# Weight loads in halves, two banks shared by two kinds of sums, and a new written order in a block of attention and spatial gating

## The chip, the cores and the metric

The kernel runs on one core of one Trainium2 chip. The metric is the device time of one execution in microseconds (us). A core has five engines with an instruction queue each: TensorE (PE in the profile; its weight loads are PEld), VectorE (DVE), ScalarE (ACT), GpSimd (POOL) and SyncE (SP), which here only issues DMAs. Engines run their queues in order and wait for each other by semaphores. TensorE writes its sums to eight banks of 128 x 512 float32, from which VectorE and ScalarE read.

## The reference

For 2048 rows of width 448, a vector c gives six modulation vectors; then an attention block and a gated mixer follow, each with a norm ahead and a residual behind:

```python
mod = (silu(c) @ w_mod)                     # sa, ca, ga, sb, cb, gb
h = layernorm(x) * (1 + ca) + sa
x = x + ga * attention(h)                   # 16 heads of 28, causal window of 256
h = layernorm(x) * (1 + cb) + sb
z = gelu(h @ w_in); z1 = z[:, :896]; z2 = layernorm(z[:, 896:])
g = w_sp @ z2 + b_sp[:, None]               # w_sp is 2048 x 2048: over the rows
x = x + gb * ((z1 * g) @ w_out)
```

All inputs and the output are bfloat16.

## The kernel before

The kernel first makes a list of operations in Python: each has a function that emits one or a few instructions (of TensorE, up to 64 matmuls), the operations that it depends on, and a claim on a buffer or a bank (`Hold`, with a `View` that lists the allowed choices). Nothing at run time chooses: a string, `PLAN`, holds one word for each operation, such as `p373.0`: the engine (p TensorE, a ScalarE, d VectorE, t GpSimd, s SP), the operation's number, and which choice each of its claims takes. `order()` reads the words from left to right, puts each operation at the end of its engine's queue, and adds a dependency on the previous holder of the claimed buffer. `count()` and `waits()` then make semaphore counts of it. So the order on each engine, the engine of an operation that could run on several, and the bank of each sum are all in that string, written once by a planner ahead of time. The numbers beside the operations (durations, priorities, `lat`) served that planner alone and do nothing when the kernel runs.

Rows are taken in 16 tiles of 128 (j, or t), and in four blocks of 512 (tb).

Front (to about 13 us): c goes through SiLU, the first modulation vectors are made, the first block of x is normed and transposed on TensorE. Small matmuls on constant data (L564) fill TensorE's waits there.

Attention. For each block, hT (transposed normed rows) comes from SP's transposing DMAs and gets its scale and shift (L731, on VectorE or GpSimd). TensorE makes Q (L762, L796), K (L820) and V (L840) into banks 6 and 7 (`bM`); they are copied out by ScalarE or VectorE (QT: L771 and L772, K: L832 and L833, V: L844 and L845). A copy of part of Q spread over zeros (QBD: L789 and L790, L814 and L815) lets one matmul serve eight heads for 64 queries. For each tile there are two halves of eight heads. Scores (L955) go to banks 0 to 3 together, and ScalarE takes their exponential (L911) into PW. Once a tile, two more matmuls make scores for eight heads (L966) in a bank of their own (`bC`, bank 5) with a short exponential (L911, 128 x 512). VectorE multiplies by the causal and window masks (L974) into PT. P.V (L1002) collects the 16 heads of a tile in one bank (`bO`, bank 4); the sums carry the softmax's denominator as a further column, so VectorE takes a reciprocal (L1016) and divides (L1018) into o_sb, which frees bank 4 for the next tile. SP transposes o_sb (`d_oT`), TensorE multiplies by w_o (L1028), VectorE adds the residual (L1032). Second norm: statistics (L628, L630, the power on GpSimd L632), the negated mean (L648), the norm (L643 or L650), a copy of its last columns (L655, L656), a transposition on SP (`d_hT`), and scale and shift for a block of four tiles (L1051 on ScalarE, L1053 on VectorE or GpSimd). w_o is scaled by ga (L600) ahead of L1028; L582 copies part of w_mod for L535.

Mixer, first half: z2 groups (L1122, GELU L1129 on ScalarE, statistics L628 and norm L1134 on VectorE), z1 groups (L1143, GELU L1151). They read w_in, which five DMAs load: three chunks of 128 rows (L432) and the last 64 rows twice (L434). Each pair of these groups needs pairs of banks (`bF`), freed by the GELUs.

Mixer, second half: w_sp @ z2 (L1168, 28 groups of 16 matmuls) with w_sp transposed by 32 DMAs from SP (`wspA` for the first half of the output rows, `wspB` for the second); VectorE adds the bias (L1172), GpSimd multiplies by z1 (L1175), TensorE multiplies by w_out (L1187), VectorE adds the residual (L1197), and SP or ScalarE stores. The first L1168 waits for all 16 z2 tiles and for wspA.

SP's queue holds loads, all transpositions and the stores in one order. An entry that waits for its source holds up those behind it.

The bank choices and the loads that the change touches:

```python
bO = View(banks, [(4,)])
bM = View(banks, [(6,), (7,)])
bC = View(banks, [(5,)])
bW = View(banks, [(0, 1, 2, 3)])
bF = View(banks, [(0, 1), (2, 3), (4, 5), (6, 7)])
```

Below stand the functions that the change touches, as a program prints them.

Of the kernel before, what the change touches and what calls it, by code (L numbers as in the profile page):

```python
# [12 lines left out]
d24 d22 p50.1 p59.3 p51.2 p58.0 p60.1 p62.0 a0 a3 a5 a7 a9 d23 d25 d26 d27 p40.1 p68.2 p74.3 p64.1 p52.0 p67.2  # L13
p53.3 p76.0 p49.3 p70.0 s1 s2 s4 d113 s6 s10 s8 a41 p45.0 p46 p47.1 p48 p73.2 p75.1 p63.2 t30 t31 t32 t35 t36
t33 d111 d114 t34 d112 t115 t37 a103 t29 t105 t38 d117.3 d116.2 p125.7 d86 d85 p128.0 p78.0 a129 a130 d106
d126 d127 d120 d121 d118 d119 a107 p83.1 p80.0 p81.1 p79.2 p77.0 p55.3 p72.2 p71.0 s12 d183 d181 p65.1 t104
p54.0 p149.1 p84.2 p140.5 p141 p150 a151 p82.1 p57.2 a142 t109 t110 t108 p137.7 p138 a139 p66.2 t122 d124.2
d123.0 p134.3 p131.6 p69.3 p56.0 p146.0 p147 p61.2 a132 d177 d184 d135 a136 s13 d243 d179 d178 d182 d180 t28
t185 t191 t187 t189 d245 d44 d241 d186.3 s11 p143.7 p370.0 a133 p164.1 p171.6 p172 d244 p165 d166 a148 p152.0
p144 d145 d173 d247 p153 d154 a371.0 p376.0 p155.1 p156 d157 a42 a377.4 p394.0 a395.1 a396 a170 t39 d380 d372  # L20
d246 d167 d374 p158.7 p159 a160 s15 p93.1 p94 d95 d248 d87 d88 d242 d397 p96.0 p97 d98 d378 s193 t188.1 s194
t190.2 s195 t192.0 s196 d197 d200 p401.0 a402.5 p174.1 p175 a176 p161.7 p162 p373.0 p89.0 p90 d91 d198 d92
a403 a43 p421.0 a422.6.0 t249 t253 d404 t251 t199 p375 p379 p381 d406 d382 d399 t252.2 d163 p217.0 p218 a219
a169 p210.1 p211 d212 p429.0 a430.0 p201.0 p202 a203 d168 p204.1 p205 a206 s14 d309 d383.2 p398.0 p400 p448.0
a449.2.1 s16 d426 s831 s258 t254.1 s259 d250.0 d255 d425 d432 d311 s384 s257 t256.3 s260 t100 t99 t261 t102
t262 t264 p226.0 p423.0 a424 p207.1 p227 p405 p208 d228 d305 p407 d408 d409.1 d306 s410 d101 d310 d431 a209
d215 d453 p456.0 p229.0 a457.1 d459 d214 d458 d452 p220.1 p221 p230 a231 p427.0 p428 s833 p475.0 p433 p434
d435 p223.0 p224 d225 d312 p450.0 a222 p232.1 d436.2 s437 d213 a476.3.2 d480 p483.0 d307 p233 d234 p235.0 p236
a451 a216 p477.0 p454.0 p455 a484.0 p501.0 d485 d486 d308 s21 s17 s834 p460 p461 d462 d479 d463.0 s464 a237
t263 p385.0 p386 d387 p411.1 p412 a478 p503.0 d413 t313 a502.6.0 p528.0 a504 d388 d505 d389 p481.0 p482 p487  # L30
p488 p271.0 p530.0 d489 d490.1 a529.2.1 d533 d506 d532 p272 a273 p509.0 a510.5 p268.1 p274.0 p275 d276 p269
d270 p507.0 p508 a531 p555.0 a556.3.2 p281.0 p265.1 p266 a267 d512 p282 p557.0 a558 a283 d511 p513 t317 t318.1
s323 t319 t320.2 s324 d314.0 s321 t315 t316.3 s322 t328 d279 d414 d560 p536.0 a537.1 p438.1 p439 d440 d280
p514 d515 d516.0 p287.0 p288 a289 p290.1 p291 a292 p563.0 a564.5 p238.0 p239 d278 p293.1 p534.0 p294 p535
p582.0 a240 p465.0 p466 d441 d442 d538 d415 d277 s20 s491 s830 s517 t390 d539 d391.2 t392 s393 a295 a583.4.0
# [215 lines left out]
def bass_adaLN_cond__sliding_block__mixer_gmlp__prompt_kernel(  # L251
# [14 lines left out]
    FH = 896  # L266
# [101 lines left out]
    sc = Sched()  # L368
    add = sc.add
    banks = Res(range(8), [])  # L370
    bO = View(banks, [(4,)])
    bM = View(banks, [(6,), (7,)])
    bA = View(banks, [(6,), (7,), (0,), (1,), (2,), (3,), (4,), (5,)])
    bL = View(banks, [(0,), (1,), (2,), (3,)])
# [325 lines left out]
    for tb in range(NB4):  # L700
# [33 lines left out]
        if tb == 0:  # L734
            for half in range(2):
                mine = {}
                for cp in range(2):
# [6 lines left out]
                    for k in range(2):  # L744
                        ch = cp + 2 * k
# [525 lines left out]
```

## Time and profile before

| | before |
|---|---|
| three timed runs | 276.37, 278.57, 280.68 us (median 278.57) |
| the profiled execution | 276.24 us |
| its span in the trace | 274.5 us |
| TensorE busy | 266.4 us (97%) |
| VectorE busy | 163.6 us (60%) |
| ScalarE busy | 121.5 us (44%) |
| GpSimd busy | 117.2 us (43%) |
| granted TensorE clock | 1.00 |

The span runs from the first instruction of the program to its last; the execution's own time has 1.7 us around it. Line numbers (L1002) are those of the kernel before, tensor names those of its program (ps: the banks). In a list of waits a row names who waited, for whom, how long in total, how often, and the longest. In the chain a row is a start, a duration and what ended last there. In a list of groups there stand line, engine, operation, output and inputs with shapes, the count, busy time in us, the mean of one in ns, and the idle time ahead. Matmuls overlap in TensorE's pipeline, so the mean of one is longer than its share of the busy time.

### The profile page before, as it was taken

The numbers are of one execution on the slowest core, as the hardware profiler recorded it, in microseconds if no ns is written. First come the engines' busy times: TensorE is split into PE (matmuls) and PEld (weight loads), VectorE is DVE, ScalarE is ACT, GpSimd is POOL, SyncE is SP. The second block draws the span as 40 slices with busy tenths as digits, with TensorE's granted clock in tenths as the row PEclk, the third lists the DMA queues.
The fourth block names the chain that finished last, engine by engine and source line by source line (L and its number), as shares of the span: only waits on it lengthen the run. The fifth ranks groups of instructions, "written<-read, shape, count | busy, mean of one in ns | idle before, by whom it ended". The sixth has DMA issues, their size and how long they took to land.

```text
span 274.5 us, 8392 instructions
## 1 busy us (share of the span) xinstructions
PE 266.4 (97%) x3741; PEld 154.1 (56%) x3751; DVE 163.6 (60%) x365; ACT 121.5 (44%) x142; POOL 117.2 (43%) x160
## 2 busy tenths in 40 slices
PE   7999998999999899999999999999999999999996
PEld 5877586678667676544544444444444444444453
DVE  3798999979899999949889301221212022153144
ACT  2599998899898789367766400000000000000000
POOL 7565467616483231488348003354453024062330
PEclk9999999999999999999999999999999999999999
DMA  7999844935431443659599996000000000001003
GB/s 216 320 222 168 109 102 116 106 94 115 114 61 43 127 61 69 175 109 155 96 173 201 191 192 112 0 0 0 2 0 0 0 2 0 33 17 52 17 33 117
DMA packets 67301, 25.54 MB, mean 93 GB/s; under 512 B 58497, under 2 KB 66178, under 8 KB 67266
## 3 DMA queue, kind: packets, MB, share of 16 engines
q1 hardware_dynamic: 66016, 24.02, 43.2%
q10 hardware_dynamic: 1250, 0.99, 1.3%
q8 instruction: 29, 0.48, 0.8%
q14 instruction: 6, 0.05, 0.1%
HBM read 9.01 MB, written 1.84 MB: 40 GB/s over the span
## 4 chain that ended last, share of the span: by engine, by line
PE 78%; DVE 12%; DMA 3%; ACT 2%; issue 2%; SPq 1%; DVEq 0%
PE ps L1168 35%; PE ps L1122 8%; PE ps L1143 8%; PE ps L1187 6%; PE ps L1002 5%; DVE PT L974 4%; PE ps L1028 4%; PE ps L820 3%; PE ps L955 3%; DMA x_sb<-in_A_x_dram 2%; PE ps L840 2%; PE ps L762 2%; DVE st_all L628 1%; DVE o_sb L1018 1%; DVE QBD L790 1%
## 5 line engine op out<-in xcount | busy, mean ns | idle before, releaser
L1175 POOL TENSOR_TENSOR z1T<-tmpg,z1T 128x512 bf16<-128x512 bf16 x28 | 32.0, 1152 | 77.7 <-DVE tmpg L1172 77.7
L1172 DVE TENSOR_TENSOR tmpg<-ps,bsp_bc 128x512 bf16<-128x512 f32 x28 | 19.0, 689 | 75.9 <-PE ps L1168 64.6
L911 ACT ACTIVATE PW<-ps 128x2048 bf16<-128x2048 f32 (+1 forms) x42 | 60.0, 1452 | 5.4 <-PE ps L955 3.7
L1168 PE MATMUL ps<-wspB,z 128*128 128x512 bf16 x219 | 49.7, 379 | 0.3
L1168 PE MATMUL ps<-wspA,z 128*128 128x512 bf16 x219 | 49.1, 379 | 0.4 <-issue 0.2
L632 POOL TENSOR_TENSOR rs_all<-mv_all,neghalf 128x1 f32<-128x1 f32 (+2 forms) x37 | 24.3, 676 | 33.1 <-DVE mv_all L630 33.1
L974 DVE TENSOR_TENSOR PT<-PW,mask 128x1024 bf16<-128x1024 bf16 x56 | 38.1, 704 | 0.2
L1168 PEld LDWEIGHTS ps<-wspA,z 128*128 128x128 bf16 x224 | 21.8, 98 | 26.6 <-issue 0.4
L1168 PEld LDWEIGHTS ps<-wspB,z 128*128 128x128 bf16 x224 | 21.9, 98 | 26.2
L1002 PE MATMUL ps<-Vaug,PT 128*128 128x32 bf16 x496 | 23.2, 177 | 1.4 <-DVE o_sb L1018 1.4
L1002 PEld LDWEIGHTS ps<-Vaug,PT 128*128 128x128 bf16 x496 | 21.3, 96 | 4.3 <-DVE o_sb L1018 2.4
L1122 PE MATMUL ps<-w_in,hT 64*128 64x448 bf16 x224 | 22.0, 349 | 0.0
L1187 PE MATMUL ps<-w_out_g,z1T 128*128 128x448 bf16 (+2 forms) x119 | 22.0, 342 | 0.0
L1143 PE MATMUL ps<-hT,w_in 64*128 64x512 bf16 x196 | 22.0, 376 | 0.0
L628 DVE BATCH_NORM_STATS2 st_all<-z 128x6 f32<-128x448 bf16 x32 | 18.4, 607 | 5.4 <-ACT z L1129 5.4
L628 DVE BATCH_NORM_STATS2 st_all<-x_sb 128x6 f32<-128x448 bf16 x32 | 19.4, 615 | 2.8 <-DMA x_sb<-in_A_x_dram 2.5
L1002 PE MATMUL ps<-Vaug,PW 128*128 128x32 bf16 x224 | 19.6, 176 | 0.0
L820 PE MATMUL ps<-hT,WQK 112*128 112x128 bf16 x256 | 17.4, 219 | 1.5 <-DVE KT L833 1.0
L1151 ACT ACTIVATE z1T<-ps 128x512 bf16<-128x512 f32 x28 | 14.6, 603 | 9.1 <-PE ps L1143 9.1
L1197 DVE TENSOR_TENSOR fin<-ps,x_sb 128x448 bf16<-128x448 f32 (+1 forms) x16 | 9.4, 611 | 14.7 <-PE ps L1187 11.4
L1002 PEld LDWEIGHTS ps<-Vaug,PW 128*128 128x128 bf16 x224 | 17.5, 96 | 1.1
L1129 ACT ACTIVATE z<-ps 128x896 bf16<-128x896 f32 x16 | 13.9, 913 | 7.9 <-PE ps L1122 5.4
(106 smaller groups left out, 351.8 us busy)
## 6 DMA issues: line engine op xcount, KB each, us to landing
wmodB<-in_w_mod_dram SPq DMA_DIRECT2D x1, 1568.0 KB, 14.7
out_dram<-fin SPq DMA_DIRECT2D x14, 112.0 KB, 1.7
x_sb<-in_A_x_dram SPq DMA_DIRECT2D x3, 448.0 KB, 7.5
w_in<-in_B_w_in_dram SPq DMA_DIRECT2D x3, 448.0 KB, 4.6
w_out_g<-in_B_w_out_dram SPq DMA_DIRECT2D x1, 784.0 KB, 5.0
bsp_bc<-in_B_b_sp_dram SPq DMA_DIRECT2D x1, 512.0 KB, 5.8
x_sb<-in_A_x_dram SPq DMA_DIRECT2D x2, 224.0 KB, 4.7
hT<-xn SPq DMA_TRANSPOSE x28, 3.0
```

Of the source, the lines that this page charges most:

```text
L628: st = [dve(0.62, lambda e, t=t, o=12 - 6 * (n - ci), s=s: e.bn_stats(st_all[:, slot, t, o:o + 6], s()), deps(t), prio) for ci, s in enume ...
L632: return pool(0.4 + 0.15 * len(tiles), lambda e: e.tensor_tensor(rs_all[:, slot, a:b], mv_all[:, slot, a:b, 1], neghalf[:, 0:b - a], ALU.pow),
L820: km = lambda g, kc, start, stop, h=h, t=t: lambda e: e.matmul(ps[:, h.slot[0], g * 128:(g + 1) * 128], lhsT=WQK[0:CP, kc, 16 + 4 * g:20 + ...
L911: ex = act(xdur, lambda e, out_ap=out_ap, in_ap=in_ap: e.activation(out_ap(), in_ap(), ACT.Exp, scale=SCALE), [s] + list(after), v - 8.0 + ...
L974: return lock_d(0.68, lambda e: e.tensor_tensor(cols(hp.slot[0] * 2048 + 1024 * k, [[256, 4], [128, 2], [1, 128]]), cols(at_w() + pad + at ...
L1002: fns.append(lambda e, hp=hp, hO=hO, hi=hi, bi=bi, kb=kb, hd=hd, nb=nb, a=at[hi][bi], p_of=p_of: e.matmul(ps[:, hO.slot[0], 32 * hd:32 * h ...
L1122: return lambda e, kc, p0, start, stop: e.matmul(ps[:, hs[t % 2].slot[hf], 0:D], lhsT=hT[p0:p0 + 64, kc, t * 128:(t + 1) * 128], rhs=w_in[ ...
L1143: return lambda e, kc, p0, start, stop: e.matmul(ps[:, hs[b // 2].slot[b % 2], :], lhsT=w_in[p0:p0 + 64, kc, ft * 128:(ft + 1) * 128], rhs ...
L1168: m = pe(16 * MMS, [lambda e, h=h, si=si, ft=ft, tb=tb: e.matmul(ps[:, h.slot[0], :], lhsT=z2[:, si, ft * 128:(ft + 1) * 128], rhs=(wspA i ...
L1172: a = dve(0.7, lambda e, h=h, ht=ht, tb=tb: e.tensor_tensor(tmpg[:, ht.slot[0], :], ps[:, h.slot[0], :], bsp_bc[:, tb * 512:(tb + 1) * 512 ...
L1175: u = pool(1.16, lambda e, ht=ht, ft=ft, tb=tb: e.tensor_tensor(z1T[tb][:, ft, :], tmpg[:, ht.slot[0], :], z1T[tb][:, ft, :], ALU.mult), [ ...
L1187: return [lambda e, ft=ft: e.matmul(ps[:, h.slot[0], 0:hi - lo], lhsT=z1T[t // 4][:, ft, (t % 4) * 128:(t % 4 + 1) * 128], rhs=w_out_g[:, ...
```

## The change

Three things are edited.

1. The three loads of 128 rows of w_in become six, each with half of the columns (0 to 895 and 896 to 1791). All readers still wait for all loads of w_in.
2. The sums of P.V (`bO`) and the scores for eight heads (`bC`) may each lie in bank 4 or 5, where before each had one bank.
3. `PLAN` is another string. The first 47 operations of TensorE, the first 13 of ScalarE, the first 18 of GpSimd and the first 11 of SP are the same, which is the front up to about 13 us. Behind it all five queues have another order, some operations another engine, and some claims another bank. From the first groups of L1168 on, TensorE and VectorE have the old order again.

The same operations are done with the same shapes, apart from the halved loads. Numbers of operations behind the loads go up by three, and line numbers behind the string by one.

By engine, the queues have these numbers of operations: TensorE 398 and 398, ScalarE 146 and 153, VectorE 365 and 376, GpSimd 156 and 138, SP 110 and 113.

```diff
 PLAN = """
-d24 d22 p50.1 p59.3 p51.2 p58.0 p60.1 p62.0 a0 a3 a5 a7 a9 d23 d25 d26 d27 p40.1 p68.2 p74.3 p64.1 p52.0 p67.2
...
+a0 t33 d27 s1 d30 d29 d28 d26 d25 p53.1 t34 p62.3 s2 t35 p54.2 t38 p61.0 s4 p63.1 p65.0 s6 a3 p43.1 a5 s10
...
 """
...
-    bO = View(banks, [(4,)])
+    bO = View(banks, [(4,), (5,)])
...
-    t_win_l = [load("d_win%d" % ch, "sp", 0.46, lambda e, ch=ch: e.dma_start(w_in[:, ch, :], B_w_in[ch * 128:(ch + 1) * 128, :]), (), -46.0 + 0.1 * ch)
-               for ch in range(3)]
+    t_win_l = [load("d_win%d%s" % (ch, "" if lo == 0 else "r"), "sp", 0.23, lambda e, ch=ch, lo=lo: e.dma_start(w_in[:, ch, lo:lo + FH], B_w_in[ch * 128:(ch + 1) * 128, lo:lo + FH]), (), -46.0 + 0.1 * ch)
+               for ch in range(3) for lo in (0, FH)]
...
-    bC = View(banks, [(5,)])
+    bC = View(banks, [(5,), (4,)])
```

123 lines of the change are left out of this document (62 added, 61 removed).

## The prediction

> **What bounds the kernel now.** I read the page first (busy time, chain by engine), then TensorE's waits, the chain in order of time, stretches, and groups of instructions by form. The page:
>
> ```profile
> span 274.5 us, 8392 instructions
> ...
> PE 266.4 (97%) x3741; PEld 154.1 (56%) x3751; DVE 163.6 (60%) x365; ACT 121.5 (44%) x142; POOL 117.2 (43%) x160
> ```
>
> TensorE is busy 97% of the span, and the diff takes none of its work away: both programs hand it the same matmuls. The time can fall only by what TensorE waits, and grows by every new wait. Its waits for other engines between 13 us, where the two programs' orders part, and 154 us, where the spatial product (L1168) starts:
>
> ```profile
> PE ps L1002 <- DVE o_sb L1018: 1.4, 2, 1.0
> PE ps L820 <- DVE KT L833: 1.0, 1, 1.0
> PE ps L925 <- ACT PT L911: 0.2, 1, 0.2
> ```
>
> Together 2.6 us, in four waits: that is what a better order behind the front can win, 0.9% of 276.24. Behind the first groups of L1168 the two programs have the same order on TensorE and VectorE, so the last 120 us only shift with the start of L1168. Where the waits sit, in the chain:
>
> ```profile
> 39.70 0.20 DVE PT L974
> 39.90 1.14 issue
> ...
> 42.49 1.07 PE ps L820 x16
> ...
> 90.77 0.46 PE ps L1002 x12
> ...
> 108.89 2.19 PE ps L1122 x22
> ...
> 144.80 9.06 PE ps L1143 x84
> ```
>
> Both long waits (ending at 42.49 and 90.77) stand behind VectorE. The 1.14 us of "issue" is a mask (L974) that took over a microsecond. From 90.77 us on TensorE is never released late. So two engines bound the middle together:
>
> ```profile
> 24.00:111.00 87.00, 84.52 (x2473) 61.44 (x2470) 82.92 (x176) 77.76 (x76) 43.05 (x53) 1.00 0.51 100
> 111.00:154.00 43.00, 42.87 (x432) 20.72 (x432) 34.78 (x91) 26.87 (x41) 25.83 (x46) 1.00 0.83 153
> ```
>
> After the length stand the busy times of PE, PEld, DVE, ACT, POOL, then the granted clock. In the attention (24 to 111 us) TensorE is busy 84.5 of 87 us, VectorE 82.9, ScalarE 77.8; in the mixer's first half VectorE has 8 us of air and ScalarE 16. The clock is 1.00 and stays out of the sum.
>
> **The change part by part.** The order view gives VectorE 11 more instructions, ScalarE 7 more, GpSimd 18 fewer. Means of the groups concerned:
>
> ```profile
> L974 DVE TENSOR_TENSOR PT<-PW,mask 128x1024 bf16<-128x1024 bf16 x56 | 38.1, 704 | 0.2
> ...
> L628 DVE BATCH_NORM_STATS2 st_all<-x_sb 128x6 f32<-128x448 bf16 x26 | 15.9, 616 | 0.2
> ...
> L790 DVE COPY QBD<-qT 32x512 bf16<-32x512 bf16 x11 | 4.0, 364 | 1.5 <-ACT qT L771 1.3
> ...
> L845 DVE CAST Vaug<-ps 128x448 bf16<-128x448 f32 x6 | 3.7, 613 | 0.1
> ...
> L772 DVE CAST qT<-ps 128x512 bf16<-128x512 f32 x4 | 2.7, 685 | 0.6 <-PE ps L762 0.6
> L1053 DVE TENSOR_SCALAR hT<-hT,modT 128x512 bf16<-128x512 bf16 x4 | 2.1, 513 | 0.0
> L833 DVE CAST KT<-ps 128x512 bf16<-128x512 f32 x3 | 2.0, 658 | 0.0
> L731 DVE TENSOR_SCALAR hT<-hT,modT 112x512 bf16<-112x512 bf16 x4 | 1.5, 399 | 0.0
> L650 DVE TENSOR_SCALAR xn<-x_sb,rs_all,nm_all 128x448 bf16<-128x448 bf16 x4 | 1.5, 374 | 0.5 <-DMA hT<-xn 0.5
> ...
> L655 DVE COPY xn<-xn 128x64 bf16<-128x64 bf16 x3 | 1.3, 443 | 0.0
> L648 DVE TENSOR_SCALAR nm_all<-mv_all,rs_all 128x1 f32<-128x1 f32 x6 | 1.2, 203 | 0.5 <-POOL rs_all L632 0.5
> ...
> L600 DVE TENSOR_TENSOR wo_g<-wo_g,gg_sb 112x448 bf16<-112x448 bf16 x1 | 0.6, 580 | 0.0
> L582 DVE COPY wmodE<-wmodB 112x512 bf16<-112x512 bf16 x2 | 0.4, 256 | 0.0
> ...
> L815 DVE COPY QBD<-qT 32x256 bf16<-32x256 bf16 x2 | 0.4, 194 | 0.0
> ```
>
> VectorE takes over from GpSimd two of L731 (0.80 us), one of L1053 (0.51), one of L600 (0.58), two of L648 (0.41), three of L650 (1.12) and four of L655 (1.77), and from ScalarE two of L815 (0.39), one of L833 (0.66) and one of L845 (0.61). It gives two of L582 (0.51) to GpSimd, two of L772 (1.37) and two of L790 (0.73) to ScalarE. Sum: 6.85 - 2.61 = +4.2 us, all ahead of L1168. How much of it lies ahead of a given instruction follows from the order view, each instruction at its group's mean:
>
> (1) The K eviction (L833) that TensorE waits for until 42.49 us; it frees one of the two banks that K has, and the next L820 needs it. Newly ahead of it on VectorE are one L628, three L648 net, one L600, two L815, two L650, one L833 and one L790, 4.0 us; no longer ahead are two L582, one L772 and one mask, 1.9 us; a pair of smaller ones cancels. So VectorE comes 2.0 us later by this count, while TensorE's matmuls ahead of that L820 are the same. Bounds for the wait: 3.0 us (1.0 now and all that is added) and 0 (if the slow mask's 1.14 us and as much again come back). I take 2.0, nearer the counted end: +1.0 us.
>
> (2) The second bank. Tile 10's sums of P.V lie in bank 4 in both programs; tile 11's go to bank 5 in the changed one, so its first L1002 no longer waits for the division (L1018) of tile 10. That takes off the wait of 1.0 us that ends at 90.77. The smaller one of its kind, 0.4 us, lies between tiles 0 and 1, which alternate now as well. Late next are the masks of tile 11, which stand beside that division in VectorE's queue; VectorE has 0.5 us more ahead of it than before. Bounds -1.4 and 0; I take -1.0. Seven of 16 tiles change bank; the others wait as now. In return the eight-head scores (L966) share a bank with sums:
>
> ```profile
> L911 ACT ACTIVATE PW<-ps 128x512 bf16<-128x512 f32 x14 | 8.4, 599 | 0.8 <-PE ps L966 0.8
> ```
>
> Their exponential keeps the bank for 0.6 us, so a P.V group right behind it would wait up to that, and none where other matmuls stand between, as the order has it: 0.
>
> (3) GpSimd's relief. Masks stretch where GpSimd works beside them; over all 56:
>
> ```profile
> L974 DVE TENSOR_TENSOR PT<-PW,mask x56: 616/682/1414, 31.1 to 110.3; 128x1024 bf16<-128x1024 bf16 x56
> ```
> ```profile
> L650 POOL TENSOR_SCALAR xn<-x_sb,rs_all,nm_all 128x448 bf16<-128x448 bf16 x17 | 14.6, 858 | 4.8 <-DVE nm_all L648 4.3
> L1053 POOL TENSOR_SCALAR hT<-hT,modT 128x512 bf16<-128x512 bf16 x11 | 8.8, 809 | 11.2 <-DMA hT<-xn 11.2
> L731 POOL TENSOR_SCALAR hT<-hT,modT 112x512 bf16<-112x512 bf16 x8 | 8.7, 1098 | 10.4 <-DMA hT<-xn 10.4
> ```
>
> Mean 704 against least 616 ns is 4.9 us of stretch. Up to 111 us GpSimd loses three L731 (3.3 us), three L650 (2.6) and small ones, some 8 of its 43 us: a fifth, so about 1.0 us of stretch comes back. Bounds 0 and 4.9; I take 1.0, half of it reaching TensorE: -0.5 us. The two L582, new on GpSimd, cost there between 0.26 us each (their VectorE row) and 0.70 (times 1098/399, L731's ratio); their reader (L535) ends no TensorE wait above. [...]
>
> (4) The end of the attention. Ahead of the last mask VectorE has 1.7 us more, less the 1.0 of (3). ScalarE has 0.7 us more ahead of the last long exponential; the last short one now stands behind it. TensorE's order puts mixer groups (L1122) between the last P.V groups as cover. Bounds 0 and +1.7; I take +0.5.
>
> (5) The mixer's first half. Six of the L1053 kind (scale and shift of the second norm) go to ScalarE.
>
> ```profile
> L1051 ACT ACTIVATE hT<-hT,modT 128x512 bf16<-128x512 bf16 x1 | 0.8, 814 | 0.0
> ```
> ```profile
> DVE st_all L628 <- ACT z L1129: 5.4, 6, 3.0
> ```
> ```profile
> 149.04 4.25 DVE L1134 TENSOR_SCALAR z<-z,mv_all,rs_all 128x896 bf16<-128x896 bf16 x10
> ```
>
> That is 4.9 us more on ScalarE, which has 16 us of air, but they queue between the GELUs that free TensorE's banks: a wait of up to 0.81 us each time, 4.9 in all, none if the spare banks hold. VectorE has 4.2 - 1.7 = 2.5 us more to do between the last mask and the last L1134, against 5.4 us in which it now waits for GELUs. Its last L1134 ends at 153.29, only 0.6 us before TensorE's L1143 does (153.86), and L1168 needs all of them. Bounds 0 and 2.5 - 0.6 = +1.9 from VectorE; I take +0.7 for both engines.
>
> (6) The w_in loads.
>
> ```profile
> w_in<-in_B_w_in_dram SPq DMA_DIRECT2D x3, 448.0 KB, 4.6
> ```
> ```profile
> w_in<-in_B_w_in_dram SPq DMA_DIRECT2D x2, 224.0 KB, 3.9
> ```
>
> Six of 224 KB for three of 448 KB: six landings of 3.9 us for three of 4.6, and three more issues on SP. The last half stands next to tile 10's o_sb transposition, which follows a division at about 91 us; the first reader of w_in is L1122 at 108.89. Cover 13 us or more, cost 0; without the cover 3 x (7.8 - 4.6) = 9.6 us at most. Transpositions behind a load wait less, but none of them ends a TensorE wait above. [...]
>
> Sum: +1.0 - 1.0 - 0.5 + 0.5 + 0.7 = +0.7 us. The profiled execution took 276.24 us (span 274.5 and 1.7 around it), so 276.9. It stands 2.3 us below the median of the three timed runs (276.37 to 280.68), and runs of the changed kernel will spread alike; halfway to the median gives 276.9 + 1.2 = 278.1 us.
>
> **The rivals.** (a) The waits go: VectorE gets its stretch back ahead of the K eviction, and the second bank takes its 1.4. Then -1.6 (a K wait of 1.0 left) to -2.6: 273.6 to 274.6 against 276.24. [...] Against it: VectorE's queue is longer at every point that I counted, by 0.5 to 4.2 us.
>
> (b) The other side: the handover to L1168 decides. VectorE's new queue puts work on landed transpositions (L650, L655, L1053) among the statistics; if one waits, all behind it waits. It costs time once VectorE is late by more than the 0.6 us above, and 2% (5.6 us) once by 6.2, that is if it keeps its 5.4 us of waits, does the 2.5 of new work and loses another 2 to 3 on landings: 282 and over. Against it: the waits of now fall on GELUs whose TensorE order is nearly the same, and the new work can fill them.
>
> (c) SP's queue.
>
> ```profile
> 135.09 7.31 SPq L465 DMA_TRANSPOSE wspA<-in_B_w_sp_dram  x5
> ...
> 143.78 1.29 SPq L465 DMA_TRANSPOSE wspA<-in_B_w_sp_dram  x1
> ```
> ```profile
> wspA<-in_B_w_sp_dram SPq DMA_TRANSPOSE x16, 4.3
> ```
>
> Between the last hT transposition and the end of wspA stand seven issues now, nine in the changed order. At up to 1.46 us each (7.31/5) the last is issued at 143.8 + 2.9 = 146.7 and lands at 151, 3 us before L1168. If the last norm is 5 us late, L1168 is 2 us late: 279.
>
> (d) The change does nothing: the waits only move: 276.2, within the forecast's range.
>
> **How the numbers follow.** Forecast (-1.0 to +2.5 around 276.9, (d) included) 0.63; (a) 0.22; (b) 0.10; (c) 0.05. Faster or slower by 2% of 278.57 is 5.6 us, about what a measurement of this kernel can tell from no change. (a) gets there only with every run at the low edge: faster 0.03. (b), and a third of (c) with runs at the high edge: slower 0.12. Within: 0.85. The range goes from (a)'s 274.6 for a run at the low edge to the forecast's +2.5 on the median, 281.1, and 0.7 for (c): 281.8.
>
> **What would show it.** In TensorE's waits: the one for L1018 near 91 us gone, the one for L833 near 42 us there and about 2 us long. VectorE's busy time up by some 3 us with the masks' mean below 704 ns; GpSimd's down by over 10. L1168 starting 0.7 us later, within -1 and +2.5. Wrong if TensorE waits for w_in, if L1168 starts past 158, or if TensorE waits over 2 us for ScalarE's share of L1053.

## The result, and the profile after

The changed kernel is slower by half a per cent: median 278.94 us over 20 runs (276.16 to 281.95) against 276.89 over 20 runs of the kernel before (275.87 to 280.68); ratio 1.0051, 95% interval 1.0026 to 1.0076, that is +1.4 us (0.7 to 2.1). The ratio leaves out the slow executions (over 1.5% above the fastest of their program: three of these 20, two of before's), so it is not that of the two medians. By the bound of 2% that is no change. The profiled execution took 280.08 us, 3.84 more than the one of before; as worked out below, 2.4 of these belong to that execution and not to the change.

Lines of the changed kernel are one higher than before (L1018 is L1019). Its page, TensorE's waits from 13 to 158 us, the masks, and the first weights of the spatial product with their first and last start:

```profile
span 278.4 us, 8397 instructions
...
PE 269.7 (97%) x3741; PEld 156.7 (56%) x3751; DVE 164.3 (59%) x376; ACT 127.4 (46%) x149; POOL 106.2 (38%) x142
```
```profile
PE ps L1123 <- ACT z L1130: 0.9, 1, 0.9
PE ps L1003 <- DVE o_sb L1019: 0.5, 1, 0.5
PE ps L821 <- DVE KT L834: 0.5, 1, 0.5
PE ps L841 <- DVE x_sb L1033: 0.4, 1, 0.4
PE ps L1003 <- issue: 0.3, 1, 0.3
PE ps L821 <- DVE Vaug L846: 0.2, 1, 0.2
PE ps L1169 <- issue: 0.2, 1, 0.2
PE ps L956 <- ACT PW L912: 0.2, 1, 0.2
```
```profile
L975 DVE TENSOR_TENSOR PT<-PW,mask 128x1024 bf16<-128x1024 bf16 x56 | 37.3, 688 | 0.5 <-ACT PW L912 0.4
```
```profile
L1169 PEld LDWEIGHTS ps<-wspA,z x224: 96/98/99, 157.7 to 226.3; 128*128 128x128 bf16 x112
```
```profile
L1168 PEld LDWEIGHTS ps<-wspA,z x224: 95/98/98, 153.8 to 222.4; 128*128 128x128 bf16 x112
```

The wait of 1.0 us near 91 us is gone, the K wait has halved to 0.5 instead of doubling, and a wait of 0.9 us in the mixer (L1123) is new. GpSimd is down by 11.0 us and ScalarE up by 5.9, but VectorE only by 0.7. The last two rows (after, before) show L1169 starting 3.9 us later. The waits have grown only from 2.6 to 3.0 us (without the row of L1169, which the kernel before has as well), so the list of waits does not tell where 3.9 us went.

What tells it is how late TensorE is. For each group of matmuls I take its start in the trace and subtract the work of all groups ahead of it, each matmul at the spacing that it has when nothing holds it (216 ns for L1168, 95 ns for L1122, 25 ns for L1002, and so on). What is left is TensorE's lateness, and only its rise between two places counts. Places are given in us of TensorE's work; its clock time is 4 to 10 us later. The profiled executions, first those with the order of before in the attention (e8, e10 and e12 are told in the text):

```
                       late  rise from .. to (us of TensorE's work)
                       at 6   6-36 36-37.5 37.5-84 84-92 92-110 110-132.5 132.5-133.5 133.5-260
before                 4.55   0.36   1.10  -1.07   0.94  -0.13    0.22     0.02       0.27
e11 before again       4.21   0.36   0.03   0.63   0.94  -0.12    0.21     0.03       0.27
e1 halves              5.34   0.52   1.26  -1.09   0.94  -0.12    0.21     0.03       0.27
e2 both banks          4.29   0.40   0.11   0.23   0.83  -0.12    0.21     0.03       0.27
e9 banks, K ahead      6.04   0.36   1.13  -0.41   0.75  -0.12    0.21     0.03       0.27
e4 new mixer           4.17   0.35   0.11   0.74   0.93   0.12    0.21     0.03       1.11
after                  6.96   0.66   0.67  -0.71   0.05   0.87    0.22     1.12       0.28
e5 after again         5.24   0.40   0.47  -0.49   0.02   1.17    0.22     1.26       0.28
e7 pair turned back    7.59   0.71   0.64  -0.73   0.15   1.34    0.22     1.43       0.29
e3 new attention       4.78   1.57   0.95  -0.02   0.03   1.45    0.22     0.03       0.26
e6 mixer mended        4.23   0.96   0.86  -0.73   0.02   1.12    0.22     0.03       0.26
e13 VectorE relieved   5.43   0.43   0.44  -0.66  -0.01   1.14    0.22     0.03       0.26
e14 ScalarE relieved   4.40   1.09   0.68  -0.73  -0.02   1.20    0.21     0.03       0.27
```

The front up to 6 us of work is the same in both programs but for VectorE's order, and there the two profiled executions differ by 2.4 us. TensorE waits 1.1 us for w_mod in after and 0.6 in before, where the last of its four loads lands at 7.8 and at 6.8 us. And its matmuls on constant data (L564 of before) start 213 ns apart until 4.6 us in both, but from 7.7 us on 109 ns in before and still 213 until 12.0 us in after; why is not shown, the granted clock is 1.00 in both. Behind the front the new order wins 0.9 us at 84-92 (the second bank), loses 1.0 to 1.6 at 92-110 (end of the attention) and 1.1 to 1.4 at 133 (last tiles of the mixer). For the two profiled executions: 2.41 in the front, 0.30 at 6-36, -0.07 at 36-84, -0.89, +1.00 and +1.10 make 3.85 of the 3.84 us.

Two sums of columns matter for what follows. Over 6-84 the new order's seven executions rise by 0.9 in the mean and the old order's six by 0.85, so up to there the orders are even. Over 84-110 the new order rises by 0.92 (after) to 1.49 and the old by 0.63 to 1.05: most of what the second bank wins at 84-92 is given back by the end of the attention. The clear loss of the change is the one at 133.

### The profile page after: what moved, and what is told of

It reads as the page before. It is cut to its first block, busy times and chain, and to the rows that moved or that the text cites. A ratio compares the mean times of both kernels' runs of the same rounds, so it can differ in the third digit from the quotient of the medians.

```text
span 278.4 us, 8397 instructions
## 1 busy us (share of the span) xinstructions
PE 269.7 (97%) x3741; PEld 156.7 (56%) x3751; DVE 164.3 (59%) x376; ACT 127.4 (46%) x149; POOL 106.2 (38%) x142
## 4 chain that ended last, share of the span: by engine, by line
PE 78%; DVE 13%; DMA 4%; ACT 3%; issue 1%; SPq 0%
PE ps L1169 35%; PE ps L1188 8%; PE ps L1144 6%; PE ps L1123 6%; PE ps L1003 5%; PE ps L956 4%; PE ps L1029 4%; PE ps L821 3%; PE ps L763 3%; DVE PT L975 3%; DVE st_all L629 2%; DMA wmodA<-in_w_mod_dram 2%; DMA hT<-xn 2%; PE ps L841 2%; ACT PW L912 1%; PE ps L565 1%
## 5 line engine op out<-in xcount | busy, mean ns | idle before, releaser
L1169 PE MATMUL ps<-wspB,z 128*128 128x512 bf16 x219 | 49.7, 379 | 0.3
L1169 PE MATMUL ps<-wspA,z 128*128 128x512 bf16 x219 | 49.1, 379 | 0.4 <-issue 0.2
L633 POOL TENSOR_TENSOR rs_all<-mv_all,neghalf 128x1 f32<-128x1 f32 (+2 forms) x37 | 25.8, 710 | 49.7 <-DVE mv_all L631 47.2
L975 DVE TENSOR_TENSOR PT<-PW,mask 128x1024 bf16<-128x1024 bf16 x56 | 37.3, 688 | 0.5 <-ACT PW L912 0.4
L1169 PEld LDWEIGHTS ps<-wspA,z 128*128 128x128 bf16 x224 | 21.8, 98 | 26.6 <-issue 0.4
L1169 PEld LDWEIGHTS ps<-wspB,z 128*128 128x128 bf16 x224 | 21.9, 98 | 26.2
L1003 PEld LDWEIGHTS ps<-Vaug,PT 128*128 128x128 bf16 x496 | 22.9, 96 | 5.3 <-issue 1.1
L1003 PE MATMUL ps<-Vaug,PT 128*128 128x32 bf16 x496 | 25.2, 177 | 0.5 <-DVE o_sb L1019 0.5
L1123 PE MATMUL ps<-w_in,hT 64*128 64x448 bf16 x224 | 22.5, 349 | 0.9 <-ACT z L1130 0.9
L1003 PE MATMUL ps<-Vaug,PW 128*128 128x32 bf16 x224 | 20.6, 176 | 0.3 <-issue 0.3
L1003 PEld LDWEIGHTS ps<-Vaug,PW 128*128 128x128 bf16 x224 | 17.8, 96 | 1.9
L821 PE MATMUL ps<-hT,WQK 112*128 112x128 bf16 x256 | 18.1, 219 | 0.7 <-DVE KT L834 0.5
L956 PEld LDWEIGHTS ps<-qT,KT 32*128 32x128 bf16 (+1 forms) x1344 | 13.4, 90 | 7.1 <-ACT PW L912 4.2
```

The costliest lines, as they stand in the source:

```text
L633: return pool(0.4 + 0.15 * len(tiles), lambda e: e.tensor_tensor(rs_all[:, slot, a:b], mv_all[:, slot, a:b, 1], neghalf[:, 0:b - a], ALU.pow),
L821: km = lambda g, kc, start, stop, h=h, t=t: lambda e: e.matmul(ps[:, h.slot[0], g * 128:(g + 1) * 128], lhsT=WQK[0:CP, kc, 16 + 4 * g:20 + ...
L956: fm.append(lambda e, hm=hm, qi=qi, key=key, kn=kn, lo=lo, hi=hi, col=col, p0=p0, t=t, j=j: e.matmul(ps[p0:p0 + kn, hm.slot[t], col:col + ...
L975: return lock_d(0.68, lambda e: e.tensor_tensor(cols(hp.slot[0] * 2048 + 1024 * k, [[256, 4], [128, 2], [1, 128]]), cols(at_w() + pad + at ...
L1003: fns.append(lambda e, hp=hp, hO=hO, hi=hi, bi=bi, kb=kb, hd=hd, nb=nb, a=at[hi][bi], p_of=p_of: e.matmul(ps[:, hO.slot[0], 32 * hd:32 * h ...
L1123: return lambda e, kc, p0, start, stop: e.matmul(ps[:, hs[t % 2].slot[hf], 0:D], lhsT=hT[p0:p0 + 64, kc, t * 128:(t + 1) * 128], rhs=w_in[ ...
```

## The experiments

Theories ahead of the first four: a Queue theory (the new order queues work behind VectorE and ScalarE), a Load theory (halved loads hold up SP), a Front theory (the new program's first loads land later). Ahead of the later ones the Queue theory is called order theory, and the landing theory says that late landings of one execution made the loss. In most experiments the written string is two lines shorter than in the changed kernel, so the attention's waits there read L1001, L819, L954 for L1003, L821, L956. Cuts of `PLAN` leave out words in between and, in places, the choice behind the point. In expectations L657, L1046 and L1055 are the pieces that the trace of the changed kernel has as L656, L1045 and L1054.

**e1: halves alone.** The changed program with one bank each and the `PLAN` of before, in which each of the three loads stands twice:

```diff
-s17 s834 ... s18 p594 ... s19 p641.0
+s17 s18 s837 ... s19 s20 p597 ... s21 s22 p644.0
```

> The order of before with the six half loads, each second half issued right behind its first. Queue theory (the +1.4 us of the changed kernel comes from waits behind VectorE and ScalarE at the end of the attention and from the last transposition of the mixer): 0 us against before, within 0.5, since no TensorE wait ends with a load. Load theory (three more loads hold up the transpositions behind them on SP's queue): +0.7 to +1.5 us. Front theory (the new program's first loads land later): 0 us.

Measured: 277.23 us, ratio 1.0002 (0.9967 to 1.0036). TensorE never waits for w_in and the table's rises are those of before. The loads cost nothing behind their cover.

**e2: the second bank alone.** `PLAN` of before, with the new choices of bank.

```diff
-    bO = View(banks, [(4,)])
+    bO = View(banks, [(4,), (5,)])
...
-    bC = View(banks, [(5,)])
+    bC = View(banks, [(5,), (4,)])
```

> The order of before, whole loads, with the bank 4 or 5 that the changed kernel gives each sum of P.V and each eight-head score. Queue theory: the TensorE wait of 1.0 us for the division (L1018) at 90.8 us goes and the small one near 31 us too; -1.0 us (between -1.4 and -0.6). Its rival, that the masks of tile 11 are late next: 0 us, with a wait of TensorE for L974 at the same place. Front theory says nothing against either.

Measured: 276.96 us, ratio 0.9996 (0.9962 to 1.0030). TensorE's waits between 84 and 95 us:

```profile
PE ps L954 <- DVE KT L832: 1.0, 1, 1.0
PE ps L1001 <- DVE o_sb L1017: 0.4, 1, 0.4
```

The wait for the division is gone, and a score (L955 of before) waits 1.0 us for a K eviction that VectorE ends at 91.91 us. The rise at 84-92 is 0.83 against 0.94: the bank alone moves the wait to the next piece in the same queue.

**e3 and e4: half of the new order each.** e3 has the new words to the end of the attention (746 of 1178), then all that is left in the order of before; e4 the reverse, with the last 426 words as in the changed kernel. Both have the halves and both banks. At e3's seam:

```diff
 s761 p778.1 s372
-p855.0 d783 a775 d737 t812 p779 p856.1
+a775 p779 t812 p855.0 p856.1 p857 d737
```

> The changed kernel up to its first mixer group (L1123 of the changed program) and the order of before for every operation left. Queue theory: the loss of 1.1 us in the mixer goes, the bank's gain (-1.1) and the loss at the end of the attention (+1.2) stay: +0.3 us against before (0 to +0.8). Front theory: as much as the changed kernel, +1.4 us, or more, as the new front is in it, and TensorE's second modulation matmuls start about 1 us later than in before.

> The order of before up to its first mixer group, then the changed order for every operation left, six half loads. Queue theory: the loss in the mixer alone, +0.9 us (+0.5 to +1.3), with a TensorE wait ahead of the mixer group of tiles 12 to 15 behind the transposition of tile 15. Front theory: 0 us or less, since the front is the one of before.

Measured: e3 277.78 us, ratio 1.0007 (0.9978 to 1.0036); e4 277.97 us, ratio 1.0012 (0.9971 to 1.0053). Neither interval excludes zero or half of the loss, but the traces part the places: e3 has the gain at 84-92 and the loss at 92-110, e4 neither. e4 lacks the loss at 133 in its profiled execution and has another one later, the bias. Waits of e4's VectorE and TensorE, 150 to 200 us:

```profile
DVE tmpg L1171 <- DMA bsp_bc<-in_B_b_sp_dram: 12.6, 1, 12.6
```
```profile
PE ps L1167 <- DVE tmpg L1171: 0.7, 1, 0.7
```

In the new order of SP the bias load stands behind seven more transposing loads of w_sp than before (28 instead of 21). VectorE waits 12.6 us for it, and TensorE waits 0.7 us for VectorE to empty a bank. In the changed kernel itself VectorE waits 11.0 us for the bias, but L1169 starts later there and TensorE does not wait.

**e5, e6, e7, e8: the new program again, and three ways to mend it.** e5 is the changed kernel. e6 makes two moves: on GpSimd the scaling of w_out goes behind the last tile's statistics, and on SP the bias load goes ahead of 16 transposing loads of w_sp:

```diff
-p1007.0 t802 t917 s798 d947 ... s850 s822 s842
+p1007.0 t917 t802 s798 s822 d947 ... s850 s842
```

e7 turns one pair of the attention's last scores and exponentials back:

```diff
-p780 ... p774 ... a781 ... a775
+p774 p780 ... a775 a781
```

e8 has the new words up to the long score of tile 13 (668 words) and then the order of before:

```diff
 a721 d578 d728
-p745.0 d529 d723 p656 p705 p369.1
+t807 d808 t529 s530 t809 s503 s681
```

> The changed kernel itself, once more, as the measure for the three others of this group and as a test of what of its loss belongs to the order and what to one execution. Order theory (the new order queues work behind VectorE and ScalarE): the profile has the same losses at the same places, TensorE 0.8 to 1.5 us later between 92 and 111 us by waits for exponentials, and L1123 waiting about 0.9 us near 143 us for L1055 behind the last transposition; median 1.0 to 1.8 us above the kernel before. Landing theory (the loss of the profiled execution was late landings, w_mod's at 7.9 us and the last hT transposition's 4.1 us): both absent in another execution, the span within 1 us of before's 274.5, median within 0.7 us of before.

> The changed kernel with two moves: the scaling of w_out (L1046) that ran on GpSimd beside the last tile's copy L657 on VectorE (1.04 beside 1.01 us) stands behind that tile's statistics, and the load of the bias goes to SP right behind the last hT transposition (it landed at 167.9 us). Order theory: L657 of tile 15 takes 0.2 to 0.4 us, the transposition starts 0.6 to 0.8 us earlier, the wait near 143 us falls from 0.9 to 0.1 or 0.3, no wait for the bias can occur; TensorE 0.7 to 1.1 us less late at 150 us than the changed kernel, median 0.7 to 1.1 us below it. Landing theory: L657 is shorter, but the wait near 143 us comes or goes with the landing (2.4 or 4.1 us) of the last transposition; median within 0.4 us of the changed kernel's.

> The changed kernel with one pair turned back to the order of before at the end of the attention: the short score of the second last tile and its short exponential (0.59 us) ahead of the long score and the long exponential (1.88 us) of the last tile. Order theory, in the form that this pair makes the loss: the rise of TensorE's lateness between 92 and 111 us falls from 0.9 to 0.4 or less, median 0.4 to 0.8 us below the changed kernel. In the form that the whole sequence from tile 13 on has too little between a score and the next: the rise stays at 0.8 to 1.2, median within 0.3 us. Landing theory: no difference outside the interval.

> The new program up to the long score of tile 13 (near 98 us), then everything that is left in the order of before; both banks, loads in halves. Order theory: it keeps the gain at tile 10 (no rise of TensorE's lateness at 86 us, -1.0) and has none of the two later losses (the rise between 92 and 111 us 0.3 or less, none near 143 us): 0.7 to 1.2 us less late at 150 us than the kernel before if the front is equal, median 0.3 to 1.0 us below before. Landing theory: equal to before within 0.4 us. Third possibility, that the early part of the new order loses as well (rises by 63 us of work, 0.4 to 0.8 in the run with the new attention): equal to before or up to 0.8 us above it.

Measured: e5 278.90 us, ratio 1.0058 (1.0026 to 1.0089); e6 277.61 us, 1.0025 (0.9986 to 1.0064); e7 278.99 us, 1.0084 (1.0050 to 1.0119); e8 280.20 us, 1.0081 (1.0039 to 1.0122).

e5 settles what belongs to the order: both late losses come back (1.17 and 1.26), the lateness of the front does not (5.24). The loss at 133 in e5, from the timelines of VectorE, GpSimd, SP and TensorE; a row is start, duration, engine, and in brackets the idle time before it:

```profile
134.49 1.01 DVE L656 COPY xn<-xn 128x64 bf16<-128x64 bf16 x1 [1.25 <-POOL xn L651]
```
```profile
134.42 1.04 POOL L1045 TENSOR_TENSOR w_out_g<-w_out_g,gg_sb 128x448 bf16<-128x448 bf16 x1
...
139.89 1.65 POOL L1054 TENSOR_SCALAR hT<-hT,modT 128x512 bf16<-128x512 bf16 x2 [3.92 <-DMA hT<-xn]
```
```profile
135.53 1.21 SPq L466 DMA_TRANSPOSE hT<-xn  x1
```
```profile
141.64 3.20 PE L1123 MATMUL ps<-w_in,hT 64*128 64x448 bf16 x32 [1.07 <-POOL hT L1054]
```

The last tile's norm ends in a copy of 64 columns on VectorE. GpSimd has just begun to scale w_out (1.04 us), and the copy starts 0.07 us later and ends with it: 1.01 us. SP issues the last transposition when the copy is done, it lands 4.3 us later, the scale and shift (L1054) follows, and TensorE has waited 1.07 us. In e6 the scaling comes later:

```profile
134.14 0.18 DVE L654 COPY xn<-xn 128x64 bf16<-128x64 bf16 x1 [1.25 <-POOL xn L649]
```
```profile
134.07 0.55 POOL L631 TENSOR_TENSOR rs_all<-mv_all,neghalf 128x1 f32<-128x1 f32 x1
134.59 1.04 POOL L1043 TENSOR_TENSOR w_out_g<-w_out_g,gg_sb 128x448 bf16<-128x448 bf16 x1
136.80 1.51 POOL L1052 TENSOR_SCALAR hT<-hT,modT 128x512 bf16<-128x512 bf16 x2 [1.17 <-DMA hT<-xn]
```

The copy takes 0.18 us, the transposition is issued at 134.35 us and lands in 2.3 us, and the wait of TensorE is gone: the rise at 133 is 0.03, and the median lies 1.3 us below e5's (0.9 by the ratios, whose intervals overlap). The order theory expected nearly this (a copy of 0.2 to 0.4 us, a median 0.7 to 1.1 below). The second move takes away VectorE's wait for the bias, but TensorE did not wait there in after or e5 either, so the rise at 133 is not its doing. The long copy stands beside the scaling in two other traces too: it began 0.06 us behind it in after and 0.07 in e4, and took 1.01 and 1.00 us. But in e6 a GpSimd instruction runs beside the copy as well (L631 above, one column, 0.55 us, begun 0.07 us earlier), and the copy does not last to its end. Why the one lengthens the copy and the other does not, the runs do not show. The landing has a part too: 4.1 to 4.4 us in after, e5 and e7, 2.3 in e6, and 2.35 in e4, where the copy took 1.00 us as well and the loss is absent. e12 below fills the last corner: it has e6's moves and a copy of 0.18 us, its landing took 3.92 us, and TensorE did not wait there either. So in these runs only a long copy and a long landing together make the loss, and mending the copy is enough. Why the landing is long in some executions and not in others stays open.

e7 changed nothing at 92-110 (1.34), so that pair is not the cause; that its ratio lies above e5's is within the intervals. e8 failed: the old order from tile 13 on meets a VectorE that is elsewhere in its queue, and TensorE waits twice for divisions, 1.1 and 1.4 us. TensorE's waits in e8, 92 to 112 us:

```profile
PE ps L1001 <- DVE o_sb L1017: 2.5, 2, 1.4
```

**e9, e10, e11: does VectorE's queue hold the stretch at 84-92?** In e9 (both banks) and e10 (one bank) the K eviction of e2's wait moves ahead in VectorE's queue, the rest as before. e11 is the kernel before.

```diff
-d649 d805 d650 ... d498 ... d341 d353
+d649 d353 d805 d650 ... d498 ... d341
```

> The order of before with the second bank (as in the run with both banks and the old order, which gained nothing because TensorE then waited 1.0 us for a K eviction at 91.9 us), and that one eviction moved ahead of three other pieces in VectorE's queue (the scale and shift L1054, the division, L644), so that it runs at 89.8 us. Theory of the late engine (the bank's gain was hidden behind the next thing in VectorE's queue): no rise of TensorE's lateness between 84 and 86 us of its work, 0.9 to 1.1 us less late than before from there on, span near 273.5, median 0.5 to 1.1 us below before. Rival (VectorE as a whole is the limit there, whatever comes first, the rest is missed later): the loss turns up again within 10 us, as a wait for the division of tile 10 or 11, its transposition or the masks, median within 0.4 us of before.

> The same move of the K eviction with one bank, as before: the division of tile 10, for which TensorE waited 1.0 us, now stands behind the eviction and ends 0.6 us later. Theory of the late engine: the wait for the division grows to 1.5 or 1.7 us, TensorE 0.4 to 0.7 us later than before, median 0.2 to 0.8 us above. Rival: no change, median within 0.3 us.

> The kernel before once more, for its first 13 us and its two waits. Landing theory: w_mod's landing and with it TensorE's lateness at 6 us of its work varies here as well (4.2 to 7 us in the programs so far), by 1 us or more against 4.6. If it belongs to the new program alone: 4.2 to 5.3 again, as in the four runs of the old front.

Measured: e9 277.82 us, ratio 1.0023 (0.9995 to 1.0051); e10 281.25 us, 1.0112 (1.0061 to 1.0162); e11, a single execution, 276.56 us. Waits of e9 between 84 and 100 us, then of e10:

```profile
PE ps L965 <- DVE o_sb L1017: 0.7, 1, 0.7
PE ps L1001 <- DVE o_sb L1017: 0.4, 1, 0.4
```
```profile
PE ps L1001 <- DVE o_sb L1017: 2.1, 2, 1.8
```

In e9 the rise at 86 us of work is gone (-0.08), and 3 us later TensorE waits 0.7 us for the next division: 0.75 in all against 0.94. The rival held: there VectorE's queue as a whole is late, and freeing one wait uncovers the next. In e10 the wait grew from 1.0 to 1.8 us, as expected, but the run lost more than that. Stretches of 2 us of e10 (the number behind POOL's is the granted clock):

```profile
94.00:96.00 2.00, 0.51 (x16) 0.51 (x17) 2.00 (x6) 0.75 (x1) 0.95 (x3) 1.00 0.38 149
96.00:98.00 2.00, 2.00 (x64) 1.77 (x61) 2.00 (x5) 0.59 (x1) 2.00 (x1) 0.54 0.30 67
98.00:100.00 2.00, 2.00 (x65) 1.59 (x49) 1.07 (x3) 1.68 (x2) 0.51 (x1) 0.60 0.45 102
```

TensorE was busy 0.51 of 2 us in its wait, and then had a granted clock of 0.54 and 0.60 for 4 us. Its lateness rises by 2.76 at 84-92 in this run, against 0.94 before; 0.8 of the difference is the longer wait, so about 1.0 us is the clock (an estimate: 2.76 - 0.94 - 0.8).

On the front, e11 lies at 4.21 again, but e9 and e10, with the front of before, at 6.04 and 8.37. The wait of after and that of e10, 4 to 13 us:

```profile
PE ps L546 <- DMA wmodA<-in_w_mod_dram: 1.1, 2, 0.9
```
```profile
PE ps L544 <- DMA wmodA<-in_w_mod_dram: 1.8, 2, 1.5
```

So TensorE leaves the front late with either program: the seven executions with the front of before (e10 included) leave it 5.3 us late in the mean, the seven with the new front in the table 5.5. The Front theory falls.

**e12: an idle time with no wait.** In e3, e5, e6 and e7 TensorE stood idle about 0.5 us (0.3 in after) inside one group of P.V at 101 to 104 us, where the program has no wait. e5's timeline:

```profile
101.28 0.18 PE L1003 MATMUL ps<-Vaug,PW 128*128 128x32 bf16 x1 [0.55 <-issue]
```

e12 is e6 with eight matmuls of one column more in TensorE's first group.

```diff
+    first = fillers[0].ways["pe"][1]
+    fillers[0].ways["pe"] = (fillers[0].ways["pe"][0], first + [lambda e: e.matmul(ps[:, 0, 0:1], lhsT=fill[:], rhs=fill[:, 0:1], start=True, stop=True)] * 8)
```

> The changed kernel with its mixer mended (as in the run of that name), and eight matmuls of one column more among TensorE's first warming ones, at its start, where it waits for w_mod anyway. In four runs with the new attention order TensorE stood idle 0.5 us near 101 us inside a group of P.V (L1003), behind the second matmul of the group, where the program has no wait; by the count of its weight loads that is load 2518. If the idle hangs on the place in TensorE's stream of instructions, it now comes eight matmuls earlier in the work, inside the long score before that group, or is gone; if it hangs on that work (what the group reads, what the other engines do at that time), it stays at the same group with 0.5 us. On the time, order theory: as the run with the mended mixer, no loss near 143 us, L657 of the last tile 0.2 to 0.4 us, median within 0.5 us of that run, 277.1 to 278.1, and 0.8 to 1.6 us below the changed kernel. Landing theory: the loss near 143 us comes back with a landing of 4 us, median as the changed kernel's.

Measured: 277.45 us, ratio 1.0021 (0.9993 to 1.0049). The idle time is gone from there and turned up nowhere else above 0.15 us. So that group's work alone does not make it; whether it hangs on the place in the stream or on the time, one run cannot say. TensorE's waits in e12 from 9 us on:

```profile
PE ps L1003 <- DVE o_sb L1019: 0.5, 1, 0.5
PE ps L821 <- ACT hT L749: 0.5, 1, 0.5
PE ps L841 <- DVE x_sb L1033: 0.4, 1, 0.4
PE ps L821 <- DVE KT L834: 0.3, 1, 0.3
PE ps L1029 <- DMA hT<-o_sb: 0.3, 1, 0.3
```

The loss at 92-110 stayed (1.16): up to 102 us of work TensorE lost nothing now (e6 had lost 0.3), and then as much more, among it a new wait of 0.3 us for the transposition of o_sb (L1029, near 107.5 us). The mended mixer held a second time, here with a landing of 3.92 us: the landing theory, by which the loss would come back with a landing of 4 us, fails.

**e13 and e14: which engine holds the end of the attention?** Both are e6 with two of the scale-and-shift pieces given to GpSimd, in e13 from VectorE, in e14 from ScalarE.

```diff
-a359 d806 p704 ... t809 t581 ... p735 d808 d777
+a359 p704 ... t806 t809 t808 t581 ... p735 d777
```
```diff
-t809 t581 t607 t582 a807 p709 ... t812 p779 ... a811 p857
+t809 t807 t581 t607 t582 p709 ... t812 t811 p779 ... p857
```

> The changed kernel with its mixer mended, and two scale-and-shift instructions of the second norm (L1055, block 0, 0.4 to 0.65 us each) taken from VectorE, where they stand among the masks of tiles 12 to 15, to GpSimd, which has half its time free there. Theory that VectorE's queue holds the end of the attention: TensorE's loss between 92 and 110 us of its work falls from 1.1 or 1.3 to 0.3 to 0.7, median 0.4 to 0.9 us below the mended run. Theory that the alternation of long score and long exponential holds it (one cannot start before the other has ended): the loss stays 1.0 to 1.3, median within 0.4 us. Theory that GpSimd's work beside the masks costs as much as it saves: masks above 720 ns between 96 and 112 us, loss 1.2 to 1.8.

> The same mended kernel with the two L1055 of blocks 0 and 1 that ScalarE got at the end of the attention (0.81 us each, one between the last two long exponentials, one behind the last short one) on GpSimd. Theory that ScalarE's added work holds the end: the loss between 92 and 110 us falls by 0.4 to 0.8, the last long exponential starts as much earlier against TensorE's work. Theory of the alternation of score and exponential: the one instruction fits between two exponentials, while TensorE makes the score, so nothing changes (loss 1.0 to 1.3) unless GpSimd is late with it, median within 0.4 us of the mended run.

Measured: e13 277.79 us, ratio 1.0010 (0.9975 to 1.0046); e14 277.47 us, 1.0002 (0.9962 to 1.0042). The rise at 92-110 is 1.14 and 1.20: neither relief does anything (e6 has 1.12). What both leave alone is the alternation of long scores and long exponentials, which share banks 0 to 3. ScalarE's exponentials in e14:

```profile
97.84 1.88 ACT L910 ACTIVATE PW<-ps 128x2048 bf16<-128x2048 f32 x1
...
100.56 2.49 ACT L910 ACTIVATE PW<-ps 128x2048 bf16<-128x2048 f32 x2 [0.41 <-PE ps L954]
...
104.27 1.88 ACT L910 ACTIVATE PW<-ps 128x2048 bf16<-128x2048 f32 x1 [0.52 <-PE ps L954]
106.99 2.37 ACT L910 ACTIVATE PW<-ps 128x2048 bf16<-128x2048 f32 x2 [0.84 <-PE ps L954]
```

Starts lie 2.72 us apart (100.56 - 97.84, 106.99 - 104.27), which is one exponential (1.88) and one score behind it; only between 100.56 and 104.27 is there more, and there the idle time lies (a row of x2 holds a short exponential behind the long one). This fits a stretch in which neither engine can run ahead. But the order of before has the same rhythm. Its long exponentials start at 88.90, 92.86, 95.76, 98.59 and 101.31 us, 2.72 to 2.90 us apart but for the first pair, where TensorE waits for the division:

```profile
88.90 1.88 ACT L911 ACTIVATE PW<-ps 128x2048 bf16<-128x2048 f32 x1 [0.28 <-PE ps L955]
...
92.86 2.37 ACT L911 ACTIVATE PW<-ps 128x2048 bf16<-128x2048 f32 x2
```

From 88.90 us on each order thus has one long gap in the same alternation, 3.96 us in before and 3.71 in e14 (100.56 to 104.27), only at another place: this agrees with a gain at 84-92 that is given back at 92-110. The alternation was not tried by itself (that would take other banks for half of the scores), and so the cause of the loss at 92-110 stays open beyond what the runs exclude as its sole cause: the pair of e7, the idle time, and the four pieces of VectorE and ScalarE that were moved.

No version was measurably faster than the kernel before. The mended ones (e6, e12, e13, e14) lie at 1.0002 to 1.0025, each with an interval that holds 1, against 1.0051 and 1.0058 for the change, whose intervals do not. The means of the two groups, 1.0015 and 1.0055, differ by 1.1 us (an estimate from these intervals, taken as independent: 0.4 to 1.8), as much as the loss in the mixer (1.1 to 1.4): most of the slowdown that can be measured is that loss.

## Why the prediction was off, step by step

The forecast was +0.7 us on the profiled execution and 278.1 for the time; measured were +1.4 (0.7 to 2.1) and 278.94. The range held it, and no run contradicts the first reading (2.6 us of waits are all that could be won).

The step that failed outright is the last one, from the sum to the time. It moved 276.9 halfway to the median of three runs, 278.57. That median stood 1.7 us above the median of 20 runs (276.89). So the 278.1, meant as 0.7 us slower, lay 0.5 us below the number that it was drawn from, and said faster; the runs showed slower by 1.4 us. In the sum itself the sign was right, in part by luck: its largest term (step 1) did not come, and the mixer brought more than was counted.

Step 1, the K wait, +1.0: failed. In the new order the rise there is 0.44 to 0.95, in the old 1.10 to 1.26 or 0.03 to 0.11 by execution. Over 36-84 the new order's seven executions in the table average +0.1 and the old order's six +0.5, and with 6-36 added the two are even (0.9 and 0.85). VectorE's added instructions ahead of an eviction did not say when TensorE would wait for it: the same program waits or does not. TensorE's lateness from the front does not tell either (the old order lost 1.13 there in e9, at 6.04, and e10, at 8.37, has no wait for K); what decides it stays open.

Step 2, the bank, -1.0: right in size where it looked (0.94 to 0.05), incomplete in its reason. e2 and e9 show that the bank by itself earns nothing that lasts, and of what the new order wins with it most is gone by 110. The smaller wait of 0.4 us, which the step put between tiles 0 and 1, ends at 86.82 us in the trace of before; in the new order 0.5 us of it is still there.

Step 3, GpSimd's relief, -0.5: mis-sized. The masks' mean of 688 ns in after is 686 in e5 but 707 in e6 and 705 in e3, against 704 to 714 in the order of before. In after that is 0.9 us over 56 masks, near the 1.0 that was counted for VectorE, but it does not come in every execution, and no run shows that it reached TensorE. The bound of 4.9 us was too wide: in before the 26 masks with no GpSimd instruction beside them took 678 ns in the mean, not 616, and the 30 others 727, which is 1.4 us of stretch in all.

Step 4, the end of the attention, +0.5: mis-sized. It measured +1.0 to +1.6, up to the end of its bounds (+1.7), and not for the pieces that were counted: moving four of them off (e13, e14) gave nothing back. Part of it is step 2's gain given back.

Step 5, the mixer, +0.7: mis-sized, and the place missed. It measured +1.1 to +1.4 at one place. The step counted queues on VectorE and ScalarE and left out who works beside whom: a copy that took 0.18 us in e6 and 1.01 in after, beside GpSimd's scaling of w_out (1.04 us), ahead of the last transposition. The wait that the trace of after names, ScalarE's GELU, is the end of that chain: it stood behind the scale and shift of the same late tile.

Step 6, the loads, 0: right (e1). What they would cost without their cover was not tried. That transpositions behind a load wait less is not shown: the row of the next one behind a load of w_in on SP's queue took 1.20 to 2.25 us in before and 1.20 to 2.93 in after.

The rivals: (a) did not come. (b) came in part: L1169 started at 157.7 us, of which 2.4 is the front. (c) came in e4, by the bias instead of wspA, with 0.7 us; in the changed kernel only VectorE waits for it. (d) did not come: the interval of the ratio excludes 1. Of the signs, the wait near 91 us and GpSimd came as told, the masks only in part; the K wait (0.5, not 2) and VectorE's busy time (+0.7, not 3) did not. The start of L1168 moved by 3.9 us, beyond its bound of 2.5; without the front it is 1.5, within it.

## What to carry to other kernels

Where one engine is full and others are busy nearly all the time beside it, a list of waits does not add up to the time: follow the full engine's lateness from place to place, over several executions, and take what only one of them has out of the account. Removing the longest wait pays only if the queue that released it is early for what comes next. In a chain that ends a stage, look at each short piece for a long instruction that another engine starts at the same moment (here the copy took 1.01 us beside one, and 0.18 in e6, where that one starts later); the move of that instruction (made together with one load) was worth most of what the whole new order had lost. And draw a forecast from the same base that the measurement will use: three runs were 1.7 us off.

## What the hardware showed that was not expected

Behind three waits of TensorE, of 1.4 to 2.4 us, the granted clock was lower. Behind the wait of 1.8 us in e10 the granted clock was 0.54 and 0.60 for 4 us (rows above). In e7 TensorE waited 2.4 us for w_mod, until 9 us, and in e8 1.4 us near 107; stretches of 2 us behind these, e7 and then e8:

```profile
8.00:10.00 2.00, 1.16 (x17) 1.16 (x18) 0.00 (x0) 0.00 (x0) 0.06 (x1) 0.84 1.12 297
10.00:12.00 2.00, 2.00 (x16) 1.75 (x15) 1.11 (x5) 0.88 (x2) 2.00 (x5) 0.50 1.09 361
12.00:14.00 2.00, 2.00 (x22) 1.68 (x21) 1.93 (x6) 1.29 (x3) 1.09 (x3) 0.80 1.17 274
```
```profile
106.00:108.00 2.00, 0.92 (x16) 0.67 (x17) 1.69 (x4) 1.73 (x1) 0.00 (x0) 0.99 0.48 106
108.00:110.00 2.00, 2.00 (x48) 1.37 (x50) 1.97 (x6) 0.00 (x0) 0.00 (x0) 0.50 0.51 115
```

Not every such wait had that: behind the 1.5 us in the front of e10 the clock stayed at 1.00, as it did behind the waits of 0.9 to 1.1 us in after. Over all executions of their groups the mean clock was below 0.995 in ten of twelve of e8 and four of six of e10, against nine of 35 and none of 17 of the kernel before. What sets these three places apart is not shown. Part of e8's loss is this clock, as an estimate: 0.50 for 2 us, and a mean of 0.993 in its profiled execution against 1.00 in before.

How late TensorE leaves the front varies by 4 us between executions that begin alike (4.2 to 8.4 us with the front of before); that is more than the change was worth. The wait for w_mod is part of it, but not alone: there was none in e5 (5.24 late), it was 0.2 us in e4 (4.17 late) and in e9 (6.04 late), 0.6 in before, 1.1 in after, 1.8 in e10 and 2.4 in e7. And the last transposition of 128 rows by SP landed in 2.3 to 2.6 us in twelve of the sixteen profiled executions and in 3.9 to 4.4 in the other four, for no reason that was found in the traces.
